# A recurrent attention block with token routing on one core: order of the tail, place of the rank sums, split of the one-hot, spread of the MLP pieces

## The chip, the core and the metric

The kernel runs on one core of a Trainium2 chip. The metric is device time in microseconds (us) for one execution, lower is better. Engines are called as in the profile: PE (TensorE, matmuls), DVE (VectorE), ACT (ScalarE), POOL (GpSimd) and SP (which only issues DMA here).

## The reference

Two blocks follow each other. The first is a linear recurrence with a decaying state per batch and head (4 batches, 8 heads, 768 steps, 48 wide):

```python
for t in range(S):
    cur = einsum('bhd,bhe->bhde', u * k[t], v[t])
    y[t] = einsum('bhd,bhde->bhe', r[t], state + cur)
    state = w * state + einsum('bhd,bhe->bhde', k[t], v[t])
```

Its output, with heads side by side, is x (4 x 768 x 384). The second block routes tokens: per batch each token gets a score, the 128 best go through an MLP, the rest is passed on.

```python
scores = x @ w_gate
for b in range(B):
    top_idx = the 128 tokens with the largest scores[b]
    h = maximum(x[b, top_idx] @ w1, 0)            # 384 -> 1024
    out[b, top_idx] = x[b, top_idx] + sigmoid(scores[b, top_idx]) * (h @ w2)
```

## The kernel before, in words

**Units.** The 768 steps of a batch are cut into 6 units of 128 tokens, 24 units in all (n = 0 to 23; batch b has units 6b to 6b+5). One loop (L562) runs over the units, and in each iteration every engine does a little of several units. Everything is scheduled by hand: each engine works through its instructions in exactly the order in which the source emits them, and waits only on semaphores. An instruction that waits therefore holds up everything emitted after it on its engine.

**One iteration n.** PE does the states' part of unit n-1 (`states`, L322), the products and scores of unit n (`products` L282, `scores` L292), the values' part of unit n-1 (`values` L338), and the transposes of unit n+1 (`turn`, L260 and L265). DVE adds the state sums (`added` L303, twice), masks the scores (`masked` L297), scales the transposed r (`turned` L275), sums the bonus (`bonus_sum` L247) and makes the token scores of unit n-1 (`score` L367). ACT copies y out (`finish` L355, L357), copies the transposed keys (L270), scales states (L310) and writes a small mark (L326) that `values` waits for. POOL does four elementwise products (L233, L251, L237, L243).

**Routing.** For unit j of batch b, PE transposes its scores so that they lie along the free axis (`scores_along`, L378), and DVE compares them with those of units 0 to j (`compare`: j+1 comparisons at L385 and one for ties at L387). After the last unit DVE sums the counts (`count`, L392), PE sums the comparisons the other way round (`rank`, L396 and L399: 16 tiny matmuls) and DVE adds both (L402, `qq`), which is every token's rank. `match` makes a one-hot matrix out of ranks, one DVE operation per unit (L423, six of them). `parts_of_scores` splits scores into bf16 parts on POOL (L410, L413). `pick` multiplies the one-hot with token numbers and scores (L429) and gives the 128 token indices (L433) and gates; `fetch` gathers their rows by an indirect DMA from POOL (L445); `chosen` transposes them (L461) and ACT copies them (L463).

**The MLP** of a batch is 16 pieces: 8 `hidden` (three matmuls each, L472; after every fourth piece ACT takes a bank through relu, L475) and 8 `expert` (one matmul each, L481), then DVE adds the result (L489) and POOL scatters it (L491). NST, the number of blocks of 128 chosen tokens, is 1 here.

**Where the side work stands.** `plan` (L519) hangs each of these on an iteration and a place in it: "scores" (behind the products and scores), "turn" (behind the transposes, ahead of `score`), "end" (last). With n the first unit after batch b, `compare` of unit j stands at n-4+j, `count` at n+1, `rank` and `match` at n+2, `pick` and `fetch` at the end of n+3, `chosen` in n+5, and the 16 MLP pieces at the ends of n+5 to n+10 by the table `MOVE` (L517): 4, 2, 2, 3, 3, 2. Each iteration from 11 on thus also carries MLP pieces of an older batch.

**One bank for much.** `scores_along`, `rank`, `pick`, `chosen`, a group of four `hidden` pieces and the eight `expert` pieces all take a PSUM tile named `m`, of which there are two. A tile is free again when its last reader has read it.

**The tail.** After the loop (L599 on) come the last unit's states and values, its scores, batch 3's rank, match, pick and fetch, and the last MLP. Left-over pieces of batch 2 are put between as filler by `some(k)`.

Of the kernel before, what the change touches and what calls it, by code (L numbers as in the profile page):

```python
# [7 lines left out]
F32 = mybir.dt.float32  # L8
BF16 = mybir.dt.bfloat16
# [3 lines left out]
OP = mybir.AluOpType  # L13
# [4 lines left out]
def kernel(  # L18
# [23 lines left out]
    nc = tc.nc  # L42
    B, H, S, D = r.shape
    C, T = 64, 128
    NC = S // T
    NU = B * NC
# [11 lines left out]
    NST = -(-cap // 128)  # L58
# [3 lines left out]
    work = ctx.enter_context(tc.tile_pool(name="work", bufs=2))  # L62
# [147 lines left out]
    slots = const.tile([128, 128], F32)  # L210
    found = const.tile([128, NC], F32)
# [100 lines left out]
    def states(n):  # L312


        YP[n] = [psum.tile([128, 512], F32, name=x) for x in ("y0", "y1")]
        for hp in range(NP):
            for j in range(2):
                for i in range(2):
                    rows = slice(i * PAD, i * PAD + D)
                    c = j ^ i  # L320
                    z = ZA[n] if c == 0 else ZB[n]
                    mm = nc.tensor.matmul(out=YP[n][i][j * C : (j + 1) * C, hp * D : (hp + 1) * D],  # L322
                                          lhsT=RH[n][rows, hp, c * C : (c + 1) * C], rhs=z[rows, hp, :],
                                          start=(hp == 0), stop=False, skip_group_check=True)
                    END[i, j] = mm
        behind = nc.scalar.copy(mark, tr[:1, 0, :1])  # L326
        for mm in END.values():
            tc.add_manual_dep(behind.ins, mm.ins.name, wait_for, reason="a mark behind the states' part")
        return behind

    def values(n, behind):

        for hp in range(NP):
            for i in range(2):
                for j in range(2):
                    c = j ^ i
# [13 lines left out]
    def finish(n):  # L350
        b, c = divmod(n, NC)
        x = xa[b][:, c, :]
        to = x.rearrange("t (p i d) -> t i p d", p=NP, i=2)
        y = [YP[n][i][:, : NP * D].rearrange("t (p d) -> t p d", p=NP) for i in range(2)]
        nc.scalar.copy(to[:, 0], y[0])  # L355
        for j in range(2):
            nc.scalar.copy(to[(1 - j) * C : (2 - j) * C, 1], y[1][j * C : (j + 1) * C])  # L357
        st = nc.sync.dma_start(out=out[b, c * T : (c + 1) * T, :], in_=x)
        for (bb, _), others in moves.items():
            if bb != b:  # L360
                for o in others:
                    tc.declare_no_dep(st.ins, o.ins, reason="rows of another batch")
        stores.setdefault(b, []).append(st)
# [4 lines left out]
                                              accum_out=sc[b][:, c : c + 1])  # L368


    SR, GT, QQ, XR, XT, IDX, GA, HT, PH, PE, OH = ({} for _ in range(11))
    spacer = const.tile([1, 1], F32)
    out_rows = out.rearrange("b s d -> (b s) d")

# [38 lines left out]
                nc.gpsimd.tensor_sub(less, rest, tok[:, at, 2 + i])  # L413
                rest = less

    def match(b, z):
        oh = OH[b, z] = work.tile([128, NC, 128], BF16, name="oh")
        q = QQ[b]
        if z:
            q = work.tile([128, NC], F32, name="qz")  # L420
            nc.vector.tensor_scalar(q, QQ[b], float(-128 * z), None, op0=OP.add)
        for c in range(NC):
            nc.vector.tensor_scalar(oh[:, c, :], slots, q[:, c : c + 1], None, op0=OP.is_equal, op1=OP.add,  # L423
                                    accum_out=found[:, c : c + 1])

    def pick(b, z):
        p = psum.tile([128, 512], F32, name="m", bufs=2)
# [78 lines left out]
    fill = {}  # L506

    def step(n, where, f, *a):
        fill.setdefault((n, where), []).append((f, a))

    def mlp(b, z):
        for f in range(FB):
            yield hidden, (b, z, f)
        for f in range(FB):
            yield expert, (b, z, f)

    MOVE = (0, 0, 0, 0, 1, 1, 2, 2, 3, 3, 3, 4, 4, 4, 5, 5)  # L517

    def plan(b):  # L519
        n = (b + 1) * NC  # L520
        for j in range(NC):
            step(n - NC + j + 2, "turn", scores_along, b, j)
            step(n - NC + j + 2, "turn", compare, b, j)
        step(n + 1, "turn", count, b)
        step(n + 2, "turn", parts_of_scores, b)
        step(n + 2, "turn", rank, b)
        for z in range(NST):
            step(n + 2, "turn", match, b, z)
            step(n + 3, "end", pick, b, z)
            step(n + 3, "end", fetch, b, z)  # L530
            step(n + 5, "scores", chosen, b, z)
        parts = [p for z in range(NST) for p in mlp(b, z)]
        for i, (f, a) in enumerate(parts):
            step(n + 5 + MOVE[i * 16 // len(parts)], "end", f, *a)

# [3 lines left out]
    def work_at(n, where):  # L539
        for f, a in fill.get((n, where), []):  # L540
            f(*a)
# [1 line left out]
    bonus(0)  # L543
    warm(10)
    pr = turn(0, k0, key_table)
    warm(4)
    load(2)
    nc.sync.dma_start(out=wg, in_=bass.AP(tensor=moe_w_gate.tensor, offset=moe_w_gate.offset, ap=[[0, 128], [1, Dm]]))
    load(3)
# [12 lines left out]
    for n in range(NU):  # L562
        if n == 2:
            late_tables()
        b, c = divmod(n, NC)
        if c == 0:
            ZA[n] = zt
        if n:
            behind = states(n - 1)
        products(n)  # L570
        scores(n)
        work_at(n, "scores")
        load(n + 4, 0, added(n, 0))
        op = masked(n)
        load(n + 4, 2, op)
        weights(2 * (n - NC), op)
        if n:
            values(n - 1, behind)
            finish(n - 1)
        if n + 1 < NU:  # L580
            pr = turn(n + 1)
        if c < NC - 1:
            added(n, 1)
        if n + 1 < NU:
            load(n + 4, 1, turned(n + 1, pr))
            load(n + 4, 3, bonus_sum(n + 1))
        if n + 2 < NU:
            scaled(n + 2)
        if n + 1 < NU:
            diagonal(n + 1)  # L590
        if n + 2 < NU:
            bonus(n + 2)
        work_at(n, "turn")
        if n:
            weights(2 * (n - NC) + 1, score(n - 1))
        work_at(n, "end")


    last = B - 1  # L599
    rest = [p for n in range(NU, NU + 2 * NC) for where in ("turn", "end") for p in fill.get((n, where), [])  # L600
            if p[0] in (hidden, expert)]
    before = [p for p in rest if p[1][0] < last]
    after = [p for p in rest if p[1][0] == last]

    def some(k):
        for _ in range(k):
            if before:
                f, a = before.pop(0)
                f(*a)

    behind = states(NU - 1)
    scores_along(last, NC - 2)
    compare(last, NC - 2)
    some(2 * NST)
    values(NU - 1, behind)
    finish(NU - 1)
    some(2 * NST)
    score(NU - 1)
    scores_along(last, NC - 1)
    compare(last, NC - 1)  # L620
# [2 lines left out]
    some(3 * NST)  # L623
    rank(last)
    for z in range(NST):
        match(last, z)
    some(2 * NST)
    for z in range(NST):
        pick(last, z)
        fetch(last, z)  # L630
    some(len(before))
    for z in range(NST):
        chosen(last, z)
    for f, a in after:
        f(*a)

# [32 lines left out]
```

## Time and profile before

| | us |
|---|---|
| median of 3 runs | 172.2 (171.87 to 173.23) |
| span of the profiled execution | 171.6 |
| PE busy | 150.7 |
| DVE busy | 123.8 |
| POOL busy | 116.7 |
| ACT busy | 72.3 |

The profile is of one execution. A row of a timeline has the start in us, the length in us, the engine, the line of the source, the operation, the tiles written and read, their shapes and how many such instructions follow each other; in brackets is how long the engine stood idle before it, and what ended that. PEld is the loading of weights into PE. A row of the windows has, for a stretch of time, its length and the busy time of PE, PEld, DVE, ACT and POOL (instructions in brackets), the clock granted to PE (1.00 is full), the busy share of the DMA engines and GB/s.

Iterations begin on PE with `states`; the row of `products` that follows is easy to find. By it iteration 7 begins at 41.53, 11 at 64.28, 12 at 72.84, 13 at 77.80, 14 at 82.75, 17 at 100.64, 18 at 108.02, 20 at 117.92 and 23 at 135.71.

### The profile page before, as it was taken

What the parts mean: (1) busy time and instruction counts of PE and PEld (TensorE: products, weight loads), DVE (VectorE), ACT (ScalarE), POOL (GpSimd) and SP (SyncE); (2) the same over time, 40 slices, a digit from 0 to 9 for tenths busy, and PEclk for the clock granted to TensorE, in tenths of its full rate; (3) what the DMA queues carried; (4) which work ended last, traced back from release to release, by engine and by line L of the source; (5) the groups of instructions that cost most, each with busy time, mean ns of one, the idle gap of its engine ahead of it and who ended that gap; (6) DMA issues with size and microseconds to landing.
All of it is one profiled execution on the core that took longest, in us unless ns stands there. A gap on an engine that the chain in (4) does not pass through costs nothing.

```text
span 171.6 us, 7987 instructions
## 1 busy us (share of the span) xinstructions
PE 150.7 (88%) x3278; PEld 123.1 (72%) x3278; DVE 123.8 (72%) x478; ACT 72.3 (42%) x227; POOL 116.7 (68%) x158
## 2 busy tenths in 40 slices
PE   7779996979896697999989999999899999967980
PEld 2468875868685586999957869999587798537840
DVE  7845877799999957769997788699976875730010
ACT  6814752546545351454535054545542543001200
POOL 8499999798998888659886979688878420231002
PEclk9978997899999858999999999999999999999999
DMA  4997887777889679999899799578101320111001
GB/s 82 209 194 139 161 193 158 160 146 154 184 204 225 143 188 263 226 213 241 202 235 227 167 225 208 120 173 182 51 4 52 97 87 8 46 46 50 0 0 46
DMA packets 84324, 24.51 MB, mean 143 GB/s; under 512 B 76480, under 2 KB 83904, under 8 KB 84288
## 3 DMA queue, kind: packets, MB, share of 16 engines
q1 hardware_dynamic: 83568, 22.42, 60.0%
q0 software_dynamic: 512, 1.57, 2.8%
q8 instruction: 26, 0.43, 1.1%
q14 instruction: 10, 0.08, 0.2%
q10 hardware_dynamic: 208, 0.00, 0.1%
HBM read 18.48 MB, written 5.51 MB: 140 GB/s over the span
## 4 chain that ended last, share of the span: by engine, by line
PE 56%; DVE 14%; issue 12%; DMA 6%; POOL 5%; ACT 4%; POOLq 1%; ACTq 0%; DVEq 0%
PE m L472 10%; PE rp L282 8%; PE m L481 7%; PE pk L260 7%; PE y L322 6%; DMA xr<-out_dram,idx 6%; PE rp L292 6%; PE y L338 6%; PE pr L265 5%; DVE rh L275 3%; ACT vpad L156 2%; DVE at L297 2%; DVE du L247 2%; DVE oh L423 2%; DVE gt L385 2%
## 5 line engine op out<-in xcount | busy, mean ns | idle before, releaser
L251 POOL TENSOR_TENSOR at<-dia,du 128x512 f32<-128x512 f32 x24 | 25.6, 1065 | 17.9 <-DVE du L247 14.9
L243 POOL TENSOR_TENSOR rku<-rk,ub 128x384 f32<-128x384 f32 x23 | 25.7, 1119 | 1.8
L385 DVE TENSOR_SCALAR_CACHE_REDUCE gt<-m,sc 128x128 bf16<-128x128 f32 x84 | 24.5, 344 | 1.9 <-PE m L378 1.9
L367 DVE SCALAR_TENSOR_TENSOR scr<-x,wg 128x384 f32<-128x384 f32 x24 | 22.0, 916 | 3.8 <-ACT x L357 1.3
L481 PE MATMUL m<-w,ht 128*128 128x384 f32 x64 | 22.8, 494 | 1.8 <-DVE qq L402 1.5
L282 PE MATMUL rp<-vpad,kw 128*48 128x96 f32 x384 | 22.1, 259 | 2.2 <-POOL kw L233 1.2
L237 POOL TENSOR_TENSOR rk<-rpad,kin 128x384 f32<-128x384 f32 x23 | 24.0, 1043 | 0.0
L472 PE MATMUL m<-xt,w 128*128 128x128 f32 x192 | 23.4, 277 | 0.6 <-ACT xt L463 0.6
L233 POOL TENSOR_TENSOR kw<-kin,wk 128x384 f32<-128x384 f32 x23 | 23.0, 1002 | 0.6 <-DMA kin<-in_k_dram 0.5
L275 DVE TENSOR_TENSOR rh<-pr,tables 112x512 f32<-112x512 f32 x24 | 16.5, 687 | 8.9 <-PE pr L265 5.0
L472 PEld LDWEIGHTS m<-xt,w 128*128 128x128 f32 x192 | 22.2, 192 | 0.9 <-ACT xt L463 0.8
L355 ACT COPY x<-y 128x192 f32<-128x192 f32 x24 | 7.6, 318 | 35.1 <-PE y L338 31.8
L310 ACT ACTIVATE z<-g,wp 128x48 f32<-128x48 f32 x80 | 20.2, 325 | 4.8 <-DVE g L303 4.8
L282 PEld LDWEIGHTS rp<-vpad,kw 128*48 128x48 f32 x384 | 16.8, 127 | 4.5 <-POOL kw L233 1.7
L322 PE MATMUL y<-g,rh 48*64 48x48 f32 x384 | 17.6, 229 | 0.6 <-issue 0.5
L297 DVE COPY_PREDICATED at<-mask,rp 128x512 f32<-128x512 uint32 x24 | 17.6, 734 | 0.7 <-POOL at L251 0.7
L292 PE MATMUL rp<-rh,kh 48*64 48x64 f32 x768 | 17.5, 231 | 0.0
L481 PEld LDWEIGHTS m<-w,ht 128*128 128x128 f32 x64 | 11.4, 190 | 8.2 <-DVE qq L402 1.9
L338 PE MATMUL y<-vpad,at 64*64 64x48 f32 x768 | 16.3, 225 | 0.4 <-ACT mark L326 0.4
L260 PE MATMUL pk<-ident,kw 128*112 128x128 f32 x92 | 16.3, 304 | 0.5 <-POOL kw L233 0.5
L322 PEld LDWEIGHTS y<-z,rh 48*64 48x64 f32 x320 | 12.3, 138 | 5.8 <-issue 3.4
L322 PE MATMUL y<-z,rh 48*64 48x48 f32 x320 | 15.2, 227 | 1.5 <-issue 1.5
(94 smaller groups left out, 254.9 us busy)
## 6 DMA issues: line engine op xcount, KB each, us to landing
rpad<-in_r_dram SPq DMA_DIRECT2D x24, 192.0 KB, 5.0
vpad<-in_v_dram SPq DMA_DIRECT2D x48, 96.0 KB, 4.1
out_dram<-x SPq DMA_DIRECT2D x24, 192.0 KB, 3.1
kin<-in_k_dram SPq DMA_DIRECT2D x23, 192.0 KB, 4.0
w<-in_moe_w_dram SPq DMA_DIRECT2D x16, 192.0 KB, 4.2
k<-in_k_dram SPq DMA_DIRECT2D x1, 192.0 KB
ub<-in_u_dram SPq DMA_DIRECT2D x1, 192.0 KB, 4.2
wg<-in_moe_w_gate_dram SPq DMA_DIRECT2D x1, 192.0 KB
```

Of the source, the lines that this page charges most:

```text
L233: nc.gpsimd.tensor_mul(kws[n % 3][:, :, :D], KIN[n], wk)
L237: nc.gpsimd.tensor_mul(rk, rpads[n % NIN][:, :, :D], KIN[n])
L243: engine.tensor_mul(RKU[n], RK[n], ub)
L251: nc.gpsimd.tensor_mul(AT[n], dia[:, None, :].to_broadcast([128, H, C]), DU[n].rearrange("t i p -> t (i p)")[:, :, None].to_broadcast([128 ...
L260: nc.tensor.transpose(pk[:CH, hp, :], two_heads(kws[n % 3] if keys is None else keys, hp), ident)
L282: nc.tensor.matmul(out=rp[i * PAD : i * PAD + D, hp // 2, at : at + 2 * D], lhsT=kws[n % 3][:, 2 * hp + i, :D], rhs=VIN[n][:, 2 * hp + i, ...
L292: nc.tensor.matmul(out=rp[ts, i, hp * C : (hp + 1) * C], lhsT=KH[n][rows, hp, ts], rhs=RH[n][rows, hp, ts], start=True, stop=True)
L322: mm = nc.tensor.matmul(out=YP[n][i][j * C : (j + 1) * C, hp * D : (hp + 1) * D], lhsT=RH[n][rows, hp, c * C : (c + 1) * C], rhs=z[rows, h ...
L338: mm = nc.tensor.matmul(out=YP[n][i][j * C : (j + 1) * C, hp * D : (hp + 1) * D], lhsT=AT[n][ts, i * NP + hp, :], rhs=VIN[n][ts, 2 * hp + ...
L385: nc.vector.tensor_scalar(GT[b][:, c, j, :], SR[b, j], sc[b][:, c : c + 1], None, op0=OP.is_gt, op1=OP.add, accum_out=counts[b % 2][:, c, ...
L472: nc.tensor.matmul(out=ph[:, f % 4, :], lhsT=w1[:, d, f * 128 : (f + 1) * 128], rhs=XT[b, z][:, d, :], start=(d == 0), stop=(d == KD - 1))
L481: nc.tensor.matmul(out=pe[:, :Dm], lhsT=HT[b, z][:, f, :], rhs=w2[:, f, :], start=(f == 0), stop=(f == FB - 1))
```

## The change

Four things are done at once.

- **Tail.** The last iteration no longer does its MLP pieces (`work_at(n, "end")` is left out there), and states, values and the copies of the last unit come first in the tail; the filler pieces come behind, in groups of 3, and one is kept until behind `chosen`. This is to bring the last unit's chain forward.
- **Rank.** `rank` moves from the "turn" of iteration n+2 to the "end" of n+1, directly behind the last unit's comparisons, so that its tile is free before the next iteration.
- **One-hot.** `match` is made in two halves of three operations, one in iteration n+2 and one in n+3, to spread DVE's work.
- **Pieces.** `MOVE` gives the MLP pieces as 3, 3, 2, 3, 3, 2. Three more warm-up matmuls (`warm(7)` for `warm(4)`) stand ahead of the loop.

```diff
-    def match(b, z):
-        oh = OH[b, z] = work.tile([128, NC, 128], BF16, name="oh")
-        q = QQ[b]
...
-        for c in range(NC):
-            nc.vector.tensor_scalar(oh[:, c, :], slots, q[:, c : c + 1], None, op0=OP.is_equal, op1=OP.add,
-                                    accum_out=found[:, c : c + 1])
+    def match(b, z, first, end):
+        if first == 0:
+            OH[b, z] = work.tile([128, NC, 128], BF16, name="oh", bufs=NST + 1)
...
+        for c in range(first, end):
+            nc.vector.tensor_scalar(OH[b, z][:, c, :], slots, QZ[b, z][:, c : c + 1], None, op0=OP.is_equal,
+                                    op1=OP.add, accum_out=found[:, c : c + 1])
...
-    MOVE = (0, 0, 0, 0, 1, 1, 2, 2, 3, 3, 3, 4, 4, 4, 5, 5)
+    MOVE = (0, 0, 0, 1, 1, 1, 2, 2, 3, 3, 3, 4, 4, 4, 5, 5)
...
+        step(n + 1, "end", rank, b)
         step(n + 2, "turn", parts_of_scores, b)
-        step(n + 2, "turn", rank, b)
         for z in range(NST):
-            step(n + 2, "turn", match, b, z)
+            step(n + 2, "turn", match, b, z, 0, NC // 2)
+            step(n + 3, "turn", match, b, z, NC // 2, NC)
...
-    warm(4)
+    warm(7)
...
-        work_at(n, "end")
+        if n + 1 < NU:
+            work_at(n, "end")
...
-    behind = states(NU - 1)
+    values(NU - 1, states(NU - 1))
+    finish(NU - 1)
     scores_along(last, NC - 2)
     compare(last, NC - 2)
-    some(2 * NST)
-    values(NU - 1, behind)
-    finish(NU - 1)
-    some(2 * NST)
+    some(3 * NST)
     score(NU - 1)
...
     for z in range(NST):
-        match(last, z)
-    some(2 * NST)
+        match(last, z, 0, NC)
+    some(3 * NST)
...
-    some(len(before))
+    some(len(before) - NST)
     for z in range(NST):
         chosen(last, z)
+    some(len(before))
```

More of the change, by code (lines that the diff above doesn't have):

```diff
@@ L368, in score @@
                                               accum_out=sc[b][:, c : c + 1])
-    SR, GT, QQ, XR, XT, IDX, GA, HT, PH, PE, OH = ({} for _ in range(11))
+    SR, GT, QQ, QZ, XR, XT, IDX, GA, HT, PH, PE, OH = ({} for _ in range(12))
     spacer = const.tile([1, 1], F32)
@@ L414, in parts_of_scores @@
                 rest = less
-    def match(b, z):
-        oh = OH[b, z] = work.tile([128, NC, 128], BF16, name="oh")
-        q = QQ[b]
-        if z:
-            q = work.tile([128, NC], F32, name="qz")
-            nc.vector.tensor_scalar(q, QQ[b], float(-128 * z), None, op0=OP.add)
-        for c in range(NC):
-            nc.vector.tensor_scalar(oh[:, c, :], slots, q[:, c : c + 1], None, op0=OP.is_equal, op1=OP.add,
-                                    accum_out=found[:, c : c + 1])
+    def match(b, z, first, end):
+        if first == 0:
+            OH[b, z] = work.tile([128, NC, 128], BF16, name="oh", bufs=NST + 1)
+            QZ[b, z] = QQ[b]
+            if z:
+                QZ[b, z] = work.tile([128, NC], F32, name="qz", bufs=NST + 1)
+                nc.vector.tensor_scalar(QZ[b, z], QQ[b], float(-128 * z), None, op0=OP.add)
+        for c in range(first, end):
+            nc.vector.tensor_scalar(OH[b, z][:, c, :], slots, QZ[b, z][:, c : c + 1], None, op0=OP.is_equal,
+                                    op1=OP.add, accum_out=found[:, c : c + 1])
     def pick(b, z):
@@ L595 @@
             weights(2 * (n - NC) + 1, score(n - 1))
-        work_at(n, "end")
+        if n + 1 < NU:
+            work_at(n, "end")
     last = B - 1
-    rest = [p for n in range(NU, NU + 2 * NC) for where in ("turn", "end") for p in fill.get((n, where), [])
+    rest = [p for n in range(NU - 1, NU + 2 * NC) for where in ("turn", "end") for p in fill.get((n, where), [])
             if p[0] in (hidden, expert)]
```

## The prediction

> **What bounds the kernel now.** I read the busy table first, then the timelines of PE, DVE and ACT over one round of six units, then windows of 3.4 us for the clock, and last the timeline of the tail.
>
> ```profile
> PE 150.7 (88%) x3278; PEld 123.1 (72%) x3278; DVE 123.8 (72%) x478; ACT 72.3 (42%) x227; POOL 116.7 (68%) x158
> ```
>
> PE leads, but not everywhere. From the 12th unit on it works without a gap; an iteration without MLP pieces is 3.5 us of PE (in the chain of waits: 0.61 + 0.80 + 0.62 + 0.45 + 0.58 + 0.44), a `hidden` piece adds 0.67 (2.68 for four), an `expert` piece 0.73 (2.20 for three). Iteration 13 starts at 77.80 and iteration 14 at 82.75: 4.95 = 3.5 + 0.11 + 1.34, nothing idle. Here every stall of PE is paid in full. PE's own timeline shows one, and the same one again at 122.20:
>
> ```profile
> 75.75 1.50 PE L472 MATMUL m<-xt,w 128*128 128x128 f32 x12
> 80.71 1.50 PE L472 MATMUL m<-xt,w 128*128 128x128 f32 x12
> 85.58 0.51 PE L399 MATMUL m<-ones,gt 128*128 128x1 bf16 x15
> 87.03 2.20 PE L481 MATMUL m<-w,ht 128*128 128x384 f32 x6 [0.77 <-DVE qq L402]
> 94.79 0.31 PE L429 MATMUL m<-tok,oh 128*128 128x5 bf16 x6
> ```
>
> The expert piece needs an `m` bank, which `rank` holds until DVE has added `qq`. DVE and ACT round these places:
>
> ```profile
> 83.22 0.35 DVE L385 TENSOR_SCALAR_CACHE_REDUCE gt<-m,sc 128x128 bf16<-128x128 f32 x1
> 94.38 0.34 DVE L387 SCALAR_TENSOR_TENSOR scr<-m,sc,earlier 128x128 f32<-128x128 f32 x1
> ```
> ```profile
> 75.83 0.59 ACT L270 COPY kh<-pk 112x512 f32<-112x512 f32 x1
> 76.31 1.01 ACT L310 ACTIVATE z<-g,wp 128x48 f32<-128x48 f32 x4
> ```
>
> 83.22 is the last comparison of batch 1's last unit (of iteration 13); ACT at 76.31 still scales states when PE has begun the hidden pieces of iteration 12.
>
> Earlier, in iterations 6 to 10, DVE is the bound (9.85 and 9.69 busy of 10 us from 40 to 60) and runs behind PE. The transpose of batch 0's last scores is done at 45.5, but its comparisons run late:
>
> ```profile
> 47.24 0.34 DVE L385 TENSOR_SCALAR_CACHE_REDUCE gt<-m,sc 128x128 bf16<-128x128 f32 x1
> 48.59 0.34 DVE L385 TENSOR_SCALAR_CACHE_REDUCE gt<-m,sc 128x128 bf16<-128x128 f32 x1
> ```
>
> The tail is a chain: ACT copies y, DVE scores, compares, ranks, matches, POOL gathers, PE runs the last MLP:
>
> ```profile
> 145.16 0.56 DVE L367 SCALAR_TENSOR_TENSOR scr<-x,wg 128x384 f32<-128x384 f32 x1 [1.32 <-ACT x L357]
> 148.97 0.17 DVE L402 TENSOR_TENSOR qq<-m,q 128x6 f32<-128x6 f32 x1 [0.60 <-PE m L399]
> ```
>
> **What the Trainium skill says.** "Trainium Kernel Development and Optimization", Best Practices: consistent bubbles can mean that PSUM ran out; the 0.77 that returns at the same place of each round, released by the op that frees an `m` bank, agrees. "DVE: scalar operands, raw-bit mode, write accounting and state across instructions", section Flops that outlive an instruction: DVE's queue is one in-order queue; the trace agrees, the comparison at 47.24 starts 1.7 us after its input, behind the older ops that fill DVE until then. "TensorE: Matmul & The Clock Gate", Part 1: the clock is halved after a window of some 3.4 us in which PE idled. The windows (PE, PEld, DVE, ACT, POOL busy, then clock) show it after one that was one third busy:
>
> ```profile
> 54.40:57.80 3.40, 1.11 (x39) 0.91 (x39) 3.29 (x9) 1.31 (x5) 3.11 (x7) 1.00 0.56 121
> 57.80:61.20 3.40, 2.95 (x89) 2.52 (x82) 3.05 (x14) 0.46 (x3) 3.08 (x4) 0.64 0.89 221
> 61.20:64.60 3.40, 3.40 (x47) 2.97 (x47) 1.47 (x5) 2.57 (x9) 2.70 (x5) 0.50 0.78 177
> ```
>
> **The change part by part**, with the waits read from the order of the built instructions.
>
> *Pieces 3,3,2.* Work is the same; 0.67 of PE moves from iterations 11 and 17 to 12 and 18. But the first four `hidden` pieces share a bank, and now it is closed in the middle of iteration 12. The next piece takes the same bank and waits for ACT's relu of it. ACT reaches that relu only after `kh` and the four `z` (end 77.32) and needs 0.60: 77.9. The fourth piece ends on PE at 75.9 + 0.67 = 76.6. PE stands 1.35, and states, products and scores of the next unit behind it. In iteration 18 `z` ends at 112.5 and the fourth piece would at 111.7: the same. Before, the relu fell into the next iteration's states and nobody waited. Two rounds: +2.7 (bounds: 2.0, if ACT's copies come earlier, to 3.0).
>
> *Rank at an iteration's end.* In iterations 13 and 19 it comes after two hidden pieces, which end at 82.21; its last five matmuls need the comparison of 83.22, done 83.57. With them PE goes on at about 83.77: +1.56. In iterations 14 and 20 the 0.77, the rank's 0.39 and the hand-over go: the experts start at 87.03, and with only the transpose (0.11) behind the turn's end at 85.61 they would at 85.72, so 1.31. Net +0.25 each, +0.5 (0 to 1).
>
> *Match in halves.* Three of six matches (0.27 apart, 0.81) move one iteration later, ahead of that iteration's comparisons. In iteration 15 the `pick` waits for the L387 of 94.38 (it takes that bank), done 94.72, just as PE arrives at 94.78. It will be done 0.81 later: PE stands 0.8 there and in iteration 21. In iteration 17 PE waits 0.41 for the gathered rows today, and that hides half of the first: +0.4 + 0.8 = +1.2 (0.6 to 1.6).
>
> *Batch 0, iterations 7 to 11.* No MLP piece stands before the rank here. PE arrives at 45.5 and waits for the comparison done at 48.93: the states of unit 7 with the products and scores of unit 8 start at 49.2 instead of 45.4. DVE, the bound, has nothing after its score (49.84) until the scores of unit 8 are there, 51.25: DVE loses 1.4. The three matches moved out give back 0.8 in iteration 8, but in iteration 9 PE must stand for the second half before `pick` (from 56.5 to 59.4), which moves unit 10 again. Followed through POOL, which does its 4.1 us of multiplications each time and holds the gather last: `tok` ends at 58.6 for 56.9, the gather starts at 63.0 instead of 61.73, +1.3 at iteration 11, where PE waits for it. That is with a full clock. PE idles 3.3 us in one piece; a half clock over iteration 8 (its pieces take 0.9 to 1.05 for 0.45 to 0.8 as at 58.6 to 65.6) adds some 2.0: +3.3. The window's phase is unknown; I take the middle, +2.3, and keep 1.0 and 3.9.
>
> *Tail.* The four hidden pieces of iteration 23 (2.68) and the six around the last unit's states and values leave its chain. DVE becomes the limit: comparisons of unit 21 end 140.83, score of 22 141.5, comparisons of 22 run 141.85 to 143.5 as today, then the score of 23 at 143.65 instead of 145.16: 1.5 earlier. The third group of fillers then costs some: three hidden pieces with a relu between (0.67 + 0.65 + 1.34) end about 147.3, after the last comparison (146.3), so `rank` starts at 147.3 for 148.39 and the index at 149.9 for 151.14: -1.25. From the gather on nothing changes but one expert piece that moves behind the transposes, under ACT's copy. If y's copies start at 138.35 instead of 139.29 (which waited by the profile for a transpose that was done), it is -2.1; PE is half idle from 138.5 to 142 and a half clock would turn it into +1.5. I take -1.3.
>
> *Three more warm-up matmuls*: 0.22 each (four take 1.03) in a gap of 1.24 before the first products, hidden; they may keep the clock up after 10.6 (0.62 in that window), but POOL is 95% busy from 10 to 20, so -0.2 (0 to -0.8).
>
> Sum: 2.7 + 0.5 + 1.2 + 2.3 - 1.3 - 0.2 = +5.2; 172.2 + 5.2 = 177.4. Ends: all favourable 2.0 + 0 + 0.6 + 1.0 - 2.1 - 0.8 = +0.7 (172.9); all unfavourable 3.0 + 1.0 + 1.6 + 3.9 + 1.5 = +11.0 (183.2). Neither end is likely at once, so I cut both.
>
> **The rivals.** (1) The stalls are absorbed and only what is removed shows: two waits of 0.77 go, the tail gains 1.3 to 2.1: 172.2 - 1.5 - 1.7 = 169.0. For it speaks that DVE is relieved by 0.8 in the iterations with most comparisons and that PE idles 1.67 + 0.76 in iteration 9 today; against it that PE has no idle time in iterations 12 and 13 to absorb 1.35 with. (2) The stalls are there but half as long (relu ready sooner, batch 0 shifted without loss): 172.2 + 1.4 + 0.3 + 0.6 + 0.5 - 2.0 = 173.0. Against it: ACT's `z` ends 0.75 after PE would be done. (3) The clock falls in batch 0 and in the tail too: 172.2 + 2.7 + 0.5 + 1.2 + 3.6 + 1.5 = 181.7. For it the windows above, against it that idle in the tail is broken up.
>
> **How the numbers follow.** Forecast 0.66, (1) 0.09, (2) 0.10, (3) 0.15. The range 173.8 to 180.8 leaves out (1), most of (2) and the most of (3). Bounds of 1% are 170.5 and 173.9: faster 0.09; same 0.10; slower 0.81.
>
> **What would show it.** Right: an idle of about 1.3 before L473 (L472 today) released by ACT `ht`, twice; idle of over 3 us before L399 near 46 released by DVE `gt`; `pick` waiting for DVE `oh` near 57 and for DVE `scr` in two later rounds; no wait for `qq` before the experts; from the last unit's score to its index about as long as today (145.2 to 151.1), but both 1.3 nearer to the start of iteration 23. Wrong: if iterations 12 and 18 last under 5.9 us the relu isn't waited for; if the first gather starts before 62, batch 0 lost nothing.

## The result and the profile after

The changed kernel takes **180.59 us** (median of 4 runs, 179.96 to 182.06); the kernel before took 172.71 beside it (171.87 to 175.57). The ratio is **1.0485, 95% interval 1.0385 to 1.0585**: slower by 4.9%. The profiled executions span 179.2 and 171.6, a difference of 7.6. Executions of one kernel fall into faster and slower ones, so here and below each time is the median of all of them, while each ratio with its interval is of the fast ones alone.

The work is the same and no engine has become the bound: the busy table of the changed kernel (us, share of the span, instructions) has 2.7 more of PE and nothing more of DVE. Of the 2.7, the warm-up matmuls are 1.3 (17 for 14), and the rank sums 0.9, because a wait inside a row of them is counted as busy.

```profile
PE 153.4 (86%) x3281; PEld 124.7 (70%) x3281; DVE 123.8 (69%) x478; ACT 72.2 (40%) x227; POOL 116.9 (65%) x158
```

So the 7.6 us are waits. To find them I took the length of each iteration on PE, from one `products` (L282) to the next, and set the two kernels beside each other. Moved work is taken out: one `hidden` piece, 0.67, left iterations 11 and 17 for 12 and 18.

| stretch | before | after | difference without moved work |
|---|---|---|---|
| start of iteration 7 | 41.53 | 40.93 | -0.60 |
| 7 to 11 (routing of batch 0) | 31.31 | 33.49 | +2.85 |
| 12 and 18 (hidden pieces) | 4.96, 4.95 | 7.14, 7.15 | +1.51, +1.53 |
| 13 + 14 and 19 + 20 (rank sums) | 11.98, 11.97 | 11.90, 11.83 | -0.08, -0.14 |
| 15 and 21 (pick) | 5.86, 5.87 | 6.67, 6.67 | +0.81, +0.80 |
| 16 and 22 | 5.00, 4.90 | 5.81, 5.83 | +0.81, +0.93 |
| 17 | 7.38 | 6.26 | -0.45 |
| 23 to the end | 35.89 | 35.52 | -0.37 |
| sum | | | +7.60 |

The rows of PE's timeline of the changed kernel that answer to those of before, iterations 12 to 16 (start, length, tiles, number of instructions, in brackets the idle time before and what ended it):

```profile
77.33 0.83 PE L473 MATMUL m<-xt,w 128*128 128x128 f32 x6
79.42 1.60 PE L473 MATMUL m<-xt,w 128*128 128x128 f32 x12 [1.26 <-ACT ht L476]
...
86.71 0.16 PE L396 MATMUL m<-ones,gt 128*128 128x1 bf16 x1 [0.69 <-ACT ht L476]
86.73 0.57 PE L399 MATMUL m<-ones,gt 128*128 128x1 bf16 x15
...
90.81 2.10 PE L482 MATMUL m<-w,ht 128*128 128x384 f32 x6
...
99.28 0.30 PE L430 MATMUL m<-tok,oh 128*128 128x5 bf16 x6 [0.81 <-DVE scr L387]
...
101.44 0.67 PE L338 MATMUL y<-vpad,at 64*64 64x48 f32 x16
102.50 0.48 PE L338 MATMUL y<-vpad,at 64*64 64x48 f32 x16 [0.39 <-issue]
```

Row two is the wait for the relu of the shared bank. The rank sums (86.71) first wait for a relu too, that of iteration 13, because they take the bank that it reads. In the row of the experts (90.81) the bracket of before, 0.77 for `qq`, is gone. `pick` waits 0.81 for the comparison L387. The last two rows were not foreseen: 32 matmuls of the values are one row of 0.63 to 0.69 elsewhere and here two, with 0.39 between them in which PE does nothing, though the profile shows nothing that it waits for.

The same view in iterations 7 to 9:

```profile
44.75 0.39 PE L399 MATMUL m<-ones,gt 128*128 128x1 bf16 x10
47.04 1.27 PE L399 MATMUL m<-ones,gt 128*128 128x1 bf16 x5 [1.90 <-DVE gt L385]
49.27 1.52 PE L282 MATMUL rp<-vpad,kw 128*48 128x96 f32 x16
50.72 1.13 PE L292 MATMUL rp<-rh,kh 48*64 48x64 f32 x32
...
60.47 0.21 PE L430 MATMUL m<-tok,oh 128*128 128x5 bf16 x3 [1.77 <-POOL tok L410]
60.85 0.71 PE L430 MATMUL m<-tok,oh 128*128 128x5 bf16 x3 [0.16 <-DVE oh L424]
```

and the windows around them (stretch, its length, busy PE, PEld, DVE, ACT, POOL, clock, DMA share, GB/s):

```profile
44.20:47.60 3.40, 0.95 (x15) 0.69 (x15) 3.40 (x14) 1.31 (x5) 2.86 (x3) 1.00 0.81 177
47.60:51.00 3.40, 3.21 (x61) 2.69 (x64) 1.76 (x12) 0.19 (x1) 3.32 (x4) 0.58 0.95 227
51.00:54.40 3.40, 3.40 (x73) 3.28 (x69) 1.23 (x3) 1.60 (x5) 0.12 (x1) 0.50 0.84 199
```

PE stands for the comparisons, is busy 0.95 of 3.40, and then runs two such stretches at about half clock; `products` takes 1.52 for 0.87. The gather of batch 0 starts at 64.96 for 61.73.

In the tail the last unit's score comes sooner, counted from the start of iteration 23 (143.68), but what follows is not shorter. Timeline of DVE of the changed kernel, and then the last row's counterpart in the kernel before:

```profile
151.78 0.56 DVE L367 SCALAR_TENSOR_TENSOR scr<-x,wg 128x384 f32<-128x384 f32 x1
156.10 0.17 DVE L402 TENSOR_TENSOR qq<-m,q 128x6 f32<-128x6 f32 x1 [1.11 <-PE m L399]
158.62 0.16 DVE L434 TENSOR_REDUCE idx<-m 128x1 int32<-128x2 f32 x1 [0.63 <-PE m L430]
```
```profile
151.14 0.16 DVE L433 TENSOR_REDUCE idx<-m 128x1 int32<-128x2 f32 x1 [0.28 <-PE m L429]
```

DVE now waits 1.11 for the rank sums (0.60 before) and 0.63 for the pick (0.28 before): PE reaches both late.

### The profile page after: what moved, and what is told of

It is laid out like the page before. It is cut to its first block, busy times and chain, and to the rows that moved or that the text cites. A ratio compares the mean times of both kernels' runs of the same rounds, so it can differ in the third digit from the quotient of the medians.

```text
span 179.2 us, 7984 instructions
## 1 busy us (share of the span) xinstructions
PE 153.4 (86%) x3281; PEld 124.7 (70%) x3281; DVE 123.8 (69%) x478; ACT 72.2 (40%) x227; POOL 116.9 (65%) x158
## 4 chain that ended last, share of the span: by engine, by line
PE 47%; DVE 14%; issue 11%; POOL 11%; SPq 6%; ACT 5%; DMA 3%; POOLq 1%; DVEq 0%; ACTq 0%
PE rp L282 7%; PE m L473 7%; PE y L322 6%; PE rp L292 6%; PE y L338 5%; PE pk L260 5%; SPq L114 5%; PE m L482 4%; DVE gt L385 4%; PE pr L265 3%; DMA kin<-in_k_dram 3%; POOL at L251 3%; POOL rk L237 3%; POOL rku L243 2%; DVE rh L275 2%
## 5 line engine op out<-in xcount | busy, mean ns | idle before, releaser
L243 POOL TENSOR_TENSOR rku<-rk,ub 128x384 f32<-128x384 f32 x23 | 26.3, 1145 | 1.8
L473 PE MATMUL m<-xt,w 128*128 128x128 f32 x192 | 24.1, 278 | 3.2 <-ACT ht L476 3.2
L233 POOL TENSOR_TENSOR kw<-kin,wk 128x384 f32<-128x384 f32 x23 | 23.0, 1000 | 0.2 <-DMA kin<-in_k_dram 0.2
L367 DVE SCALAR_TENSOR_TENSOR scr<-x,wg 128x384 f32<-128x384 f32 x24 | 21.3, 886 | 2.2
L282 PE MATMUL rp<-vpad,kw 128*48 128x96 f32 x384 | 22.1, 261 | 0.7 <-POOL kw L233 0.6
L303 DVE TENSOR_TENSOR g<-rp,z 128x192 f32<-128x192 f32 x20 | 7.1, 354 | 17.8 <-PE rp L292 17.8
L282 PEld LDWEIGHTS rp<-vpad,kw 128*48 128x48 f32 x384 | 17.0, 129 | 2.6 <-POOL kw L233 1.1
L322 PEld LDWEIGHTS y<-z,rh 48*64 48x64 f32 x320 | 13.0, 141 | 7.6 <-issue 3.9
L338 PE MATMUL y<-vpad,at 64*64 64x48 f32 x768 | 17.1, 223 | 1.2 <-issue 0.8
L322 PE MATMUL y<-z,rh 48*64 48x48 f32 x320 | 16.3, 231 | 2.0 <-issue 1.0
L292 PEld LDWEIGHTS rp<-rh,kh 48*64 48x64 f32 x768 | 14.2, 141 | 3.4 <-issue 0.5
```

The costliest lines, as they stand in the source:

```text
L233: nc.gpsimd.tensor_mul(kws[n % 3][:, :, :D], KIN[n], wk)
L243: engine.tensor_mul(RKU[n], RK[n], ub)
L292: nc.tensor.matmul(out=rp[ts, i, hp * C : (hp + 1) * C], lhsT=KH[n][rows, hp, ts], rhs=RH[n][rows, hp, ts], start=True, stop=True)
L367: return nc.vector.scalar_tensor_tensor(scr, xa[b][:, c, :], 1.0, wg, op0=OP.mult, op1=OP.mult, accum_out=sc[b][:, c : c + 1])
L473: nc.tensor.matmul(out=ph[:, f % 4, :], lhsT=w1[:, d, f * 128 : (f + 1) * 128], rhs=XT[b, z][:, d, :], start=(d == 0), stop=(d == KD - 1))
```

## The experiments

Each kernel computes the whole reference. Ratios are to the kernel before on the same chip. "Iteration" is as in the table.

### The pieces back, and a bank of its own for each group

`u_pieces` is the changed kernel with the old table of pieces.

```diff
-    MOVE = (0, 0, 0, 1, 1, 1, 2, 2, 3, 3, 3, 4, 4, 4, 5, 5)
+    MOVE = (0, 0, 0, 0, 1, 1, 2, 2, 3, 3, 3, 4, 4, 4, 5, 5)
```

> The changed kernel with one part undone: the pieces per iteration are 4,2,2,3,3,2 again. Theory: iterations 12 and 18 last 7.14 and 7.15 us where 5.63 would be the work, because the fourth hidden piece closes a bank and the fifth waits for its relu, so this gives back 2 x 1.5 = 3.0 us: about 177.6 us, and the idle ahead of the hidden pieces released by ACT is gone from the loop. Rival (a plain shift of work between iterations, the loss lies elsewhere): no change, 180.6 us.

178.33 us, ratio 1.0338 (1.0255 to 1.0422), span 176.6. Iterations 12 and 18 take 4.95 and 4.95, for 7.14 and 7.15; the piece of 0.67 that went back to the iteration before explains the smaller part, and each is 1.5 better beyond it. `banks` keeps the 3, 3, 2 and gives each group a bank and a relu of its own:

```diff
-        if f % 4 == 0:
+        groups = ((0, 3), (3, 6), (6, 8)) if b < B - 1 else ((0, 4), (4, 8))
+        lo, hi = [g for g in groups if g[0] <= f < g[1]][0]
+        if f == lo:
             PH[b, z] = psum.tile([128, 4, 128], F32, name="m", bufs=2)
...
-        if f % 4 == 3:
-            nc.scalar.activation(HT[b, z][:, f - 3 : f + 1, :], ph, AF.Relu)
+        if f == hi - 1:
+            nc.scalar.activation(HT[b, z][:, lo:hi, :], ph[:, : hi - lo, :], AF.Relu)
```

> The changed kernel, pieces 3,3,2 kept, but the hidden pieces of batches 0 to 2 take a bank for 3, 3 and 2 of them, so that no bank is closed in the middle of an iteration and the relu (three instead of two for a batch) falls behind the iteration's pieces. Theory: the 1.5 us in iterations 12 and 18 are the wait for the relu of the shared bank and nothing else, so both last 5.6 to 5.7 us and the time falls by 3.0 us (and up to 0.4 in the tail, where a relu stood between fillers): 177.4 us. Rival (the third piece in iterations 12 and 18 costs that time in itself): no change, 180.6 us.

179.35 us, ratio 1.042 (1.0108 to 1.0732), span 177.9; iterations 12 and 18 take 5.62: the 4.95 of before and the one piece of 0.67. PE's rows of iteration 12 in `banks` are one group without a bracket:

```profile
78.31 2.17 PE L475 MATMUL m<-xt,w 128*128 128x128 f32 x18
```

The wait belongs to the bank that is closed after one piece of the iteration, not to the number of pieces. The whole gains less than the 3.0 expected, 1.3 in span: in this execution iteration 7 starts 0.6 later than in the changed kernel, iterations 7 to 11 take 0.4 more, and the tail has a half clock that costs 0.8.

### The rank sums back, for all batches and for batch 0 alone

```diff
-        step(n + 1, "end", rank, b)
         step(n + 2, "turn", parts_of_scores, b)
+        step(n + 2, "turn", rank, b)
```

> The changed kernel with one part undone: the rank sums stand among the turn's work of iteration n+2 again. Theory: only batch 0 paid for it (the changed kernel's iterations 7 to 11 took 2.85 us more), batches 1 and 2 came out even (1.33 more in iterations 13 and 19, 1.4 less in 14 and 20): about -2 us, 178.6 us, with a full clock in iteration 8. Rival (the price is paid in every batch, as the prediction had it, 0.25 each, on top of batch 0): -2.8 us, 177.8 us, and iterations 13 plus 14 together shorter than the 11.9 us of the changed kernel.

178.68 us, ratio 1.0324 (1.0227 to 1.0421), span 177.5. Iteration 7 is 4.79 again for 8.34, and 7 to 11 take 31.12 for 33.49, though a half clock remains in them. For the later batches nothing is gained: iterations 13 and 14 take 4.95 + 7.02 = 11.97, as before; at the end of n+1 they took 11.90. PE's rows show the old wait back:

```profile
86.44 0.51 PE L399 MATMUL m<-ones,gt 128*128 128x1 bf16 x15
87.88 2.20 PE L482 MATMUL m<-w,ht 128*128 128x384 f32 x6 [0.77 <-DVE qq L402]
```

`rank0` separates the two: only batch 0 goes back.

```diff
-        step(n + 1, "end", rank, b)
+        if b:
+            step(n + 1, "end", rank, b)
         step(n + 2, "turn", parts_of_scores, b)
+        if not b:
+            step(n + 2, "turn", rank, b)
```

> The changed kernel with the rank sums of batch 0 alone back among the turn's work; batches 1 to 3 as in the changed kernel. Theory: iteration 7 falls from 8.3 to 4.8 us, the clock stays full in iteration 8 and batch 0's gather starts at about 60.3 us as when all ranks stood there; iterations 13 and 14 stay 6.3 and 5.55 us: together the gain of the run in which all ranks stood there, 1.9 us less, 178.7 us. Rival (batches 1 and 2 gave a part of that gain): half of it, 179.7 us.

177.66 us (one of its five executions took 747.36), ratio 1.0342 (a wide interval, 1.003 to 1.0654), span 174.5. Iterations 7 to 11 take 29.46, 4.0 less than in the changed kernel; 13, 14, 19 and 20 are unchanged but for 0.07 in 14. `u_rank` does the same work up to iteration 12, on another chip, and took 31.12, with more of it at half clock. So the place of the rank sums costs 2.4 to 4.0 in batch 0 and next to nothing in the others. No gain of the halved one-hot is seen there: four kernels with the one-hot whole and the rank sums as before (`tail1`, `tail2`, `best1`, `best2`, below) take 30.1 to 30.3, or 29.5 to 29.6 less the moved piece.

### The one-hot whole again, and the gather moved away from the values

```diff
-            step(n + 2, "turn", match, b, z, 0, NC // 2)
-            step(n + 3, "turn", match, b, z, NC // 2, NC)
+            step(n + 2, "turn", match, b, z, 0, NC)
```

> The changed kernel with one part undone: the one-hot is made whole in iteration n+2. Theory: the wait before the pick (0.81 us in iterations 15 and 21) goes, and with it the 0.9 us that iterations 16 and 22 lost in the values' matmuls, because the gather no longer falls on them; the first gather wait of 0.4 comes back: about -2.9 us, 177.7 us. Rival (the prediction's step, the pick's wait alone): -1.2 us, 179.4 us, with iterations 16 and 22 as long as in the changed kernel (5.8 us).

Iterations 15 and 21 fall to 6.17 and 6.16, and 16 and 22 to 4.91 and 4.91: 1.4 in each round, and two thirds of it in the iteration behind the pick. Yet the time is 180.52 (ratio 1.0424, 1.032 to 1.0527; span 179.4), so the whole doesn't show the gain of 2.9 that was expected. In the profiled execution iteration 11 took 10.87 for 6.31, where PE stood 3.00 for the gathered rows and had the half clock after, and the tail 1.35 more. I don't put the first down to the one-hot: in the seven kernels in which PE waits at this place, 4.5 to 5.9 us pass from the start of the gather to the use of its rows, and it was longest in `best3` below, which has the one-hot whole and the rank sums of batch 0 as before. Why it varies stays open.

Why do 16 and 22 gain? The timeline of all engines of the changed kernel in iteration 16 shows it:

```profile
101.22 1.02 POOL L446 DMA_INDIRECT xr<-out_dram,idx  x1 [0.16 <-issue]
101.38 0.60 PEld L338 LDWEIGHTS y<-vpad,at 64*64 64x64 f32 x16
101.44 0.67 PE L338 MATMUL y<-vpad,at 64*64 64x48 f32 x16
...
102.50 0.48 PE L338 MATMUL y<-vpad,at 64*64 64x48 f32 x16 [0.39 <-issue]
102.71 0.36 DVE L303 TENSOR_TENSOR g<-rp,z 128x192 f32<-128x192 f32 x1 [2.40 <-PE rp L292]
...
102.99 0.32 ACT L355 COPY x<-y 128x192 f32<-128x192 f32 x1 [2.35 <-PE y L338]
```

POOL issues the gather from 101.22 to 102.24 (the expectations call this the making of descriptors; the trace shows how long POOL takes for it, not what it does). At 102.11 PE stops in the middle of the values until 102.50, and DVE starts `added` at 102.71 although the scores ended at 101.61 (100.92 + 0.69). POOL's own stream is as before: its gather starts 7.76 behind the start of iteration 15 (7.75 before). PE's isn't: having waited 0.8 at the pick it begins iteration 16 that much later. Before, the gather lay 1.89 behind the start of iteration 16 (97.53 for 95.64) and fell on the end of the values and the transposes; now it lies 1.09 behind it, on the values. The kernel before at that place:

```profile
97.00 0.68 PE L338 MATMUL y<-vpad,at 64*64 64x48 f32 x32
97.53 1.03 POOL L445 DMA_INDIRECT xr<-out_dram,idx  x1 [0.15 <-issue]
97.61 0.65 PE L260 MATMUL pk<-ident,kw 128*112 128x128 f32 x4
```

`gather` tests this by the place of the gather alone, behind the next unit's L233 on POOL:

```diff
-            step(n + 3, "end", fetch, b, z)
+            step(n + 4, "scaled", fetch, b, z)
...
             scaled(n + 2)
+        work_at(n, "scaled")
```

> The changed kernel with the gather of the chosen rows behind POOL's next product (L233), about 1 us later than in the changed kernel, for all batches but the last. Theory: while POOL makes the gather's descriptors (1.03 us), what PE signals to DVE and ACT arrives late and PE itself stops after some small matmuls; 1 us later it falls on the turn's transposes and the MLP pieces, so iterations 16 and 22 last 5.0 instead of 5.8 us: 1.6 us less, unless the rows then come late at iteration 17: 179.0 to 179.4 us. Rival (those 0.9 us are a wait for the mark behind the gate on ACT): no change in iterations 16 and 22.

Iteration 16 falls from 5.81 to 4.91, iteration 22 stays at 5.83. The second is a control that I hadn't planned: in iteration 22 there is no unit 24 to scale, so no L233 stands ahead of the gather and it did not move. Timelines of `gather`, iteration 16 and then 22:

```profile
100.78 1.00 POOL L233 TENSOR_TENSOR kw<-kin,wk 128x384 f32<-128x384 f32 x1
...
101.24 0.63 PE L338 MATMUL y<-vpad,at 64*64 64x48 f32 x32
101.55 0.36 DVE L303 TENSOR_TENSOR g<-rp,z 128x192 f32<-128x192 f32 x1 [1.44 <-PE rp L292]
...
101.97 1.03 POOL L446 DMA_INDIRECT xr<-out_dram,idx  x1 [0.15 <-DVE g L303]
...
137.82 1.03 POOL L446 DMA_INDIRECT xr<-out_dram,idx  x1 [0.15 <-issue]
138.04 0.69 PE L338 MATMUL y<-vpad,at 64*64 64x48 f32 x18
139.14 0.46 PE L338 MATMUL y<-vpad,at 64*64 64x48 f32 x14 [0.41 <-issue]
139.34 0.36 DVE L303 TENSOR_TENSOR g<-rp,z 128x192 f32<-128x192 f32 x1 [2.42 <-PE rp L292]
```

With the gather behind the values they are whole and DVE starts 0.1 after the scores (100.72 + 0.69 = 101.41); with the gather on them both are late. As a version it is no gain: 182.2 us (180.24 to 185.34), span 179.1, since its tail had the half clock (36.54) and iterations 7 to 11 took 0.9 more than in the changed kernel.

### The tail

`u_tail` is the changed kernel with the old tail, and with four pieces of batch 2 in iteration 23 as before; `tail1` is the kernel before with the new tail alone (the tail's part of the change's diff).

```diff
-        if n + 1 < NU:
-            work_at(n, "end")
+        work_at(n, "end")
...
-    values(NU - 1, states(NU - 1))
-    finish(NU - 1)
+    behind = states(NU - 1)
     scores_along(last, NC - 2)
     compare(last, NC - 2)
-    some(3 * NST)
+    some(2 * NST)
+    values(NU - 1, behind)
+    finish(NU - 1)
+    some(2 * NST)
...
```

> The changed kernel with the tail of before (iteration 23 does four hidden pieces, the fillers stand as before). Theory: the new tail brings 0.4 to 0.5 us only, because the fillers between comparison and pick hold up rank and pick: 181.0 us. Rival (the prediction's 1.3 us from the last unit's earlier score): 181.9 us.

> The kernel before with the new tail alone; everything up to iteration 23 as before, so iteration 23 starts on PE near 135.7 and its part to the end says what the new tail is worth (35.89 before, 35.52 in the changed kernel). Theory (the filler pieces put ahead of the rank sums and of the pick take back most of what the earlier scores gain): 35.4 to 35.6, the span 171.2, the ratio 0.997. Rival (the forecast's term, 1.3 less): 34.6, the span 170.3. Second rival (PE is partly idle around the last values, and the clock is halved): over 36.3, the span 172 or more.

`u_tail`: 181.74 us, ratio 1.0527 (1.0424 to 1.0629), iteration 23 to the end 37.60, where the same tail took 35.89 in the kernel before. Step for step the two agree up to the gathered rows; then the last eight hidden pieces take 7.25 for 5.62, because the clock is halved behind the idle time before those rows (windows of `u_tail`):

```profile
159.80:163.20 3.40, 1.18 (x6) 0.35 (x5) 0.62 (x1) 0.48 (x1) 1.21 (x4) 1.00 0.30 93
163.20:166.60 3.40, 3.40 (x16) 3.40 (x17) 0.00 (x0) 0.00 (x0) 0.00 (x0) 0.52 0.09 27
```

In the kernel before the same stretch (153.0 to 156.4, busy 1.20) was followed by full clock. `u_tail` therefore doesn't price the tail. `tail1` does: 174.72 us, ratio 1.0045 (1.0000 to 1.0090), and 35.83 for 35.89: the new tail alone is worth nothing. Where it goes is seen by cutting iteration 23 to the end into steps (us):

| | before | tail1 | after | best1 | tail2 | best2 |
|---|---|---|---|---|---|---|
| start to the last score | 9.45 | 8.41 | 8.10 | 8.51 | 8.47 | 7.96 |
| to `qq` | 3.81 | 4.33 | 4.32 | 4.45 | 3.66 | 3.66 |
| to the index | 2.17 | 2.52 | 2.52 | 2.16 | 2.16 | 2.16 |
| to `chosen` | 3.64 | 3.77 | 3.77 | 4.55 | 3.78 | 3.78 |
| to the end | 16.82 | 16.80 | 16.81 | 16.86 | 16.87 | 16.78 |
| sum | 35.89 | 35.83 | 35.52 | 36.53 | 34.94 | 34.34 |

In `tail1` the score gains 1.0; the fillers ahead of the rank sums take back 0.5 and those ahead of the pick 0.35. The 0.5 is a closed bank again: of the three pieces there the first closes a bank, and the second waits for its relu (`tail1`):

```profile
145.39 1.60 PE L472 MATMUL m<-xt,w 128*128 128x128 f32 x12 [0.69 <-ACT ht L475]
```

`tail2`, below, also has three pieces there, but its bank is closed earlier, and `qq` follows the score after 3.66. Five of the eight kernels with the new tail (`u_pieces`, `u_match`, `u_rank`, `banks`, `gather`) also had the half clock behind the last values and took 36.34 to 36.87; the three without it (`after`, `rank0`, `tail1`) 35.52 to 35.83.

### Versions from the parts that help

`best1` is the kernel before with `warm(7)`, the rank sums of batches 1 to 3 behind the scores of iteration n+2 (so that `qq` is there before the experts, and batch 0 stays as it was), and the new tail with fillers of 1, 3, 2, 2.

```diff
-        step(n + 2, "turn", rank, b)
+        step(n + 2, "scores" if b else "turn", rank, b)
...
-    warm(4)
+    warm(7)
...
```

> The kernel before with what the runs leave as good: the three more warm-up matmuls, ranks of batches 1 and 2 behind the products and scores of iteration n+2 (so that the bank is free before the experts and no comparison is waited for), pieces and one-hot as before, and the tail with the last unit first and fillers of 1, 3, 2, 2 and the rest. Theory: 1.0 us from the start of the loop, 2 x 0.77 us from the waits for qq, 1.0 us from the tail: 171.6 less 3.5 in span, about 169.2 us. Rival (the start of the loop is given back at the first gather, and PE's work bounds the tail): 0.9 us less than before at most, 171.5 us.

171.0 us, ratio 0.9902 (0.9858 to 0.9945), span 169.2. Iterations 14 and 20 take 6.20 for 7.03 (no wait for `qq`), of which 15 and 21 give back 0.3 each, since PE now comes earlier to the same L387. Its tail is the worst of the table: after a stretch with PE busy 2.18 of 3.40 the clock was halved from 139 to 143.

`tail2` is `best1` with fillers 2, 2, 3, 2. `best2` is `tail2` with the scatter of batch 1 issued behind the last gather (`LATE` keeps it until there, and `idx` has one more buffer). `best3` is the scatter, the rank and the warm-up of `best2` with the tail of before. The fillers of `tail2` and, in the last lines, the late scatter of `best2`:

```diff
-    some(1)
+    some(2)
     values(NU - 1, states(NU - 1))
...
-    some(3)
+    some(2)
     score(NU - 1)
...
-    some(2)
+    some(3)
     rank(last)
...
         fetch(last, z)
+    for b, z, ot in LATE:
+        leave(b, z, ot)
```

> As best1 (rank behind the scores of iteration n+2 for batches 1 to 3, seven warm-up matmuls), with fillers 2, 2, 3, 2 in the tail for 1, 3, 2, 2. best1 had the half clock from 139 to 143 after a window in which PE was busy 2.18 of 3.40; the piece moved ahead of the last states fills that window. Theory: its half clock (1.44 for three pieces) goes, half of the moved piece's 0.67 is paid: iteration 23 to the end 35.4 for 36.53, the span 168.1. Rival: the clock's window falls elsewhere and a half clock returns: 36.5, the span 169.2.

> tail2 with the scatter of batch 1 issued from POOL behind the last gather instead of in iteration 22 (one more idx buffer for it). In best1 this scatter's descriptors (134.91 to 135.94) lay over the last values but one, and ACT's copy of y began at 136.31 and the comparisons at 136.41, though PE was done with both at 135.25 and 135.5. Theory (POOL's making of descriptors holds up the signals between PE, ACT and DVE): the comparisons of unit 21 start within 0.3 of the transposition's end, the chain of scores runs 0.8 earlier: iteration 23 to the end 34.6, the span 167.3. Rival (ACT and DVE were late for another reason): the gap stays 0.8, the time as tail2.

> Rank behind the scores of iteration n+2 for batches 1 to 3, seven warm-up matmuls and the later scatter, with the tail of the kernel before. There PE is the limit from the transposition of unit 21 to that of unit 22 (four hidden pieces and the states between), so comparisons that start 0.8 earlier are worth nothing. Theory: iteration 23 to the end 35.9 as before, the span 168.6. Rival (the scatter held up PE's own work too): 35.1, the span 167.8; or the clock halves over the last hidden pieces as in u_tail: 37.5, the span 170.2.

`tail2`: 170.95 us, ratio 0.9734 (0.9657 to 0.9811), span 168.0, no half clock in its tail, which takes 34.94 (35.4 expected). `best2`: **169.34 us, ratio 0.9772 (0.9716 to 0.9828)**, span 166.6, tail 34.34. The times don't separate these two, and no more is claimed than that both beat both kernels; the traces do separate what the scatter does. In `tail2` the scatter runs from 135.28 to 136.31 and DVE's comparisons of unit 21 start 0.84 late, released by a transposition that PE had finished at 135.90:

```profile
135.28 1.03 POOL L491 DMA_INDIRECT out_dram<-ot,idx  x1 [1.35 <-DVE g L303]
136.66 0.32 ACT L355 COPY x<-y 128x192 f32<-128x192 f32 x1 [1.10 <-PE m L378]
136.75 0.35 DVE L385 TENSOR_SCALAR_CACHE_REDUCE gt<-m,sc 128x128 bf16<-128x128 f32 x1 [0.84 <-PE m L378]
```

`best2` has no scatter there, and at the same place (the values end at 134.84, the transposition at 135.10) neither engine stands:

```profile
134.88 0.32 ACT L355 COPY x<-y 128x192 f32<-128x192 f32 x1
135.14 0.35 DVE L385 TENSOR_SCALAR_CACHE_REDUCE gt<-m,sc 128x128 bf16<-128x128 f32 x1
```

`best3` has the same two starts without a wait (138.22 and 138.48), yet its iteration 23 to the end is 35.99, as expected no better than 35.89: with the old tail PE has no idle time there (busy 3.40 of 3.40 from 136.0 to 139.4), so DVE's earlier start is worth nothing. 172.3 us, ratio 0.9865 (0.9806 to 0.9925). Its profiled execution (171.6) lost some 4 us in iteration 11, with a wait of 3.20 for batch 0's rows; the other five, without a trace, span 168.5 to 171.6.

## Why the prediction was partly wrong

The direction and most mechanisms were right, the size was not: 177.4 was forecast, 180.59 came, near the upper end of the range. Two steps failed: the halved one-hot, where nothing was counted behind the pick, and in the tail the way from the rank sums to the index. By its terms, in us of the profiled executions:

| term | forecast | measured | shown by |
|---|---|---|---|
| pieces 3, 3, 2 | +2.7 | +3.04 | `u_pieces`, `banks` |
| rank sums, batches 1 and 2 | +0.5 | -0.22 | table, `u_rank` |
| match in halves | +1.2 | +2.90 | `u_match`, `gather` |
| batch 0 | +2.3 | +2.85 | `rank0`, `u_rank` |
| tail | -1.3 | -0.37 (-0.06 alone) | `tail1` |
| warm-up, up to iteration 7 | -0.2 | -0.60 | table only |
| sum | +5.2 | +7.60 | |

- **Pieces.** Right in cause and place. The step was 1.35 a round, it measured 1.51 and 1.53: the piece was done at 77.33 + 0.67 = 78.00, ACT came to the relu, behind its copy and scalings, at 78.79, and PE went on at 79.42.
- **Rank sums.** The wait came where the text put it, but in two parts: first 0.69 before L396 for ACT's relu, whose bank the rank sums take, which the text did not see, and then the comparison that it named. The second sets the end: in `banks` the relu is shorter, and what PE no longer stands for it, it stands inside the row of L399 (0.83 for 0.57), and iteration 13 is 6.28 in both:

```profile
85.91 0.16 PE L396 MATMUL m<-ones,gt 128*128 128x1 bf16 x1 [0.47 <-ACT ht L478]
85.93 0.83 PE L399 MATMUL m<-ones,gt 128*128 128x1 bf16 x15
```

Iterations 13 and 19 lost 1.33 instead of 1.56 and 14 and 20 gained 1.41 and 1.47 instead of 1.31. What is gained there is partly lost at the next pick: with the one-hot whole, PE still waits 0.31 for L387 (`u_match`). So this term and the next share the waits before the pick, and the table's split between them is one of several.

- **Match in halves, the step that failed.** It counted the halves only where the pick waits for them: 0.81 and 0.80 in iterations 15 and 21 (0.4 and 0.8 said, the 0.45 of iteration 17 counted apart). That was right. It put nothing on iterations 16 and 22, which lost 0.81 and 0.93: PE, late by the wait, met the gather of its own batch on POOL in the values. These 1.74 are all that this term was short by.
- **Batch 0.** The idle before L399 was there (1.90 in the bracket, and some 1.1 more within the row of five, which takes 1.27 where ten take 0.39), and so was the half clock behind it. The forecast had 1.3 without and 3.3 with the half clock and took the middle; the half clock came, as in all six kernels that have these rank sums at the end of iteration 7, and it measured 2.85. That is against one trace of before, which was long here: against the 30.1 to 30.3 of the four kernels named above the loss is 3.8 to 4.0.
- **Tail, the second step that failed.** The score's gain was read nearly rightly (1.5 said, 1.35 measured, 9.45 to 8.10), and so were the three pieces before the rank sums, relu included: `rank` was to start 1.09 earlier and starts 0.84 earlier, counted from the start of iteration 23. "From the gather on nothing changes" held but for 0.1. Wrong was the way from the start of `rank` to the index, 2.6 in the text and 2.75 before: it took 3.10, since PE comes to the pick behind three pieces instead of two, and nothing was counted for that. So of the 1.25 said at the index 0.49 was left. Nor did it see that the scatter holds up the tail's first copies and comparisons; it took the 0.85 before them for something that the change might remove.
- **Rivals.** The third (half clock in batch 0 and in the tail, 181.7) is nearest by time. Its first half is in this trace; its second isn't, though five of eight kernels with this tail had it, at a cost of 0.8 to 1.4 (36.34 to 36.87 for 35.52).
- **What would show it**: the waits for ACT `ht`, DVE `gt` and DVE `scr` are there, the `qq` wait is gone. The pick of batch 0 waits for POOL `tok` (1.77) ahead of DVE `oh` (0.16), which was not foreseen.

That the extra warm-up matmuls give the earlier start of iteration 7 was not tried alone. The kernels with seven start it at 39.9 to 41.5, those with four (`before`, `tail1`) at 41.5 and 41.3. The clock right behind the warm-up does go with them: in the two windows from 10.2 to 17.0 it is 0.62 and 0.88, and 0.77 and 0.72, with four, and 1.00 in all twelve kernels with seven.

## What to carry to other kernels

Where one engine has no idle time left, a bank that is closed in the middle of a stretch makes it wait for the reader's whole queue; close it at the stretch's end, or give the first part its own bank (7.14 to 5.62 here). When a wait moves one engine against another that doesn't share it, look at what the two then do at the same time: here the second loss was as large as the wait itself, and came from an indirect DMA that was issued over small matmuls. Filler work on a critical engine has to be sized to the gap of each wait, not to the sum of the gaps, and a shared bank should not close inside it.

## What was not expected of the hardware

**While POOL issues an indirect DMA, other engines are held up.** The issue takes POOL 0.97 to 1.18 us. What waited for PE in that time started on DVE and ACT only 0.35 to 0.75 after its end in the two places shown (102.24 to 102.71 and 102.99; 136.31 to 136.66 and 136.75), and PE itself stopped among small matmuls (0.39 in the changed kernel, 0.41 in `gather`). Moving the gather (`gather`, iteration 16 from 5.81 to 4.91) and the scatter (`best2`, DVE's wait of 0.84 to none) removed this both times. By what path POOL does it stays open.

**The same idle time of PE can be followed by a half clock or by a full one.** In `u_rank` and in the changed kernel the same work, with the same busy time in PE (1.91 and 1.93 of 3.40), was followed by half clock in one and full clock in the other (windows of each):

```profile
143.05:146.45 3.40, 1.91 (x70) 1.42 (x69) 2.59 (x13) 1.62 (x5) 0.91 (x1) 1.00 0.23 86
146.45:149.85 3.40, 3.40 (x44) 3.31 (x44) 1.89 (x15) 0.95 (x3) 0.00 (x0) 0.50 0.24 87
```
```profile
145.60:149.00 3.40, 1.93 (x70) 1.44 (x69) 2.60 (x13) 1.61 (x5) 0.93 (x1) 1.00 0.23 84
149.00:152.40 3.40, 2.92 (x51) 2.68 (x51) 2.42 (x16) 0.95 (x3) 0.00 (x0) 1.00 0.26 94
```

So 0.8 to 1.7 us can come or go in a later stretch that an edit doesn't touch, and a tail is priced over several kernels rather than from one. What decides it isn't shown, and it need not be the edit: each kernel has one trace, and `rank0` and `u_rank`, with the same work up to iteration 12, had different clocks from 47.6 to 64.6.
